# A second layer of seven products for one more block of four rounds, an earlier first FFT stage, and logits copied on ScalarE

## The chip, the cores and the metric

The kernel runs on one core of a Trainium2 chip. A core has five engines with a queue of instructions each: TensorE (PE, matrix products; its weight loads are shown apart as PEld), VectorE (DVE), ScalarE (ACT), GpSimd (POOL) and SyncE (SP, which issues most transfers here). Operands lie in SBUF, 128 partitions wide; products land in PSUM. The metric is the device time of one execution in microseconds. It was 1263.31 us before the change, the median of three runs (1263.24 to 1265.31).

## The reference

The input `x` has 8 batches of 2496 rows of 256 numbers. First the real part of a two-dimensional Fourier transform of each batch; then a layer of eight experts, of which each row takes the one with the greatest logit.

```python
X = np.fft.fft(x, axis=1)
X = np.fft.fft(X, axis=2)
x = X.real.astype(np.float32).reshape(B * S, D)        # 19968 x 256

logits = x @ w_gate                                    # 256 x 8
expert_idx = np.argmax(logits, axis=1)
probs = np.exp(logits - logits.max(-1, keepdims=True))
probs /= probs.sum(-1, keepdims=True) + 1e-09
gate_w = probs[np.arange(N), expert_idx]
for e in range(E):                                     # the rows of expert e
    h = np.maximum(x_sorted[lo:hi] @ w1[e], 0.0)       # 256 -> 1024
    y_sorted[lo:hi] = h @ w2[e]                        # 1024 -> 256
return gate_w[:, None] * y                             # in the order of the rows
```

No row is dropped: an expert's share of rows depends on the data, so the kernel finds out on the chip which rows go to which expert.

## The kernel before

**The transform** of a batch has two stages. The first, `first(b)`, goes through three thirds of the batch: a transfer brings `xq` (L289), DVE folds it (`fold`, with L295 to L297 in `fold_d` and L306), TensorE multiplies (`s`, L316 on), ScalarE copies the result (`t`, L321), and SP writes it to `Td` in HBM (L342). `regroup` (L351) reads it back in another order, as two tiles `t`. The second stage, `second(b)`, turns one column (`turn_last`: a product `pr`, and the copy `t` by ScalarE on L372), runs nine groups (`group`: two products `p` from `t` and the table, and ScalarE's copy `zz`, L379), and from these ten tiles of 128 places: two products `p` from `zz`, ScalarE's copy `zs` (L405), ScalarE's `mirror` (L384), the copy of the logits `lg` (L408), and two additions on DVE into `rows` (L410). Each place gives two rows of the transform. After five tiles `route` (L416) finds each row's expert, gate and place; `send` then writes rows to their places in the sorted array `Xs` in HBM by an indirect transfer on POOL (L236), 128 rows each, behind two tiny copies (ScalarE's `due`, L468, and POOL's cast, L469).

**The plan.** When a batch has been routed, `plan` (L478) works out on one partition of DVE how many full blocks of rows each expert has, and writes a table of where each block begins and whose weights it takes. Its arrays have 21 entries (`MOST`), the greatest number of blocks that any call plans. SP reads the table and fetches rows (`fetch_rows`, L526) and weights (`fetch_weights`, L542), up to three blocks ahead.

**The experts** go in rounds, one per batch. From batch 2 a round has blocks of 512 rows: three in round 2, five in rounds 3 to 6; round 7 has five and then smaller ones. A block, written (round, index), has two layers. The plain form of the first layer is a chain of products `ph`, that of the second 4 times 16 products `py` with a scaling by ScalarE (L891) and an indirect store after each. Blocks for which `halved` holds (512 rows from round 3 on) run the first layer as seven products of half the size in place of eight (`seven`, L614; products a to e; Strassen's scheme), for which DVE prepares sums of the weights (`Left`, L552) and of the turned rows (`right`, L568, called by `turn`, L577, which also transposes on L583 and negates on ScalarE on L586). Blocks for which `quartered` holds run the second layer so too: `lower` (L660), with the sums of weights by `Below` (L594, its subtractions on L607; on POOL for blocks of 512) and sums of the hidden tile by DVE (chores on L819 at the end of `seven`, `s2` on L870, `s4` on L874). In `lower` DVE adds the products (L705, L707, L713 and `plus`, L683) and ScalarE scales them (`scaled`, L679). `Below` of a block is begun during the block before if that one's second layer is direct (`soon`, L855), else in the block's own first layer. `quartered` holds for index 3 and 4 of rounds 3 to 6 and for the whole of round 7.

**The order.** Every engine's queue is in the order in which the program was written; nothing is reordered later. The main loop (L996 on) goes through the steps of the experts' work (`work`), and after each takes some ticks from the side work, `mixed(b)` (L935): the first stage of batch b + 1 (`ahead_of`) and the second stage of batch b, then the plans (`close`). So a round's blocks carry the transform of the next batches between their products: a generator step of the first stage comes with every second step of the second. 12 further ticks (`AHEAD`) of the round after next come at the end of a round, and in rounds 3 to 5 they fall into the second layer of index 2. PSUM gives the transform three banks (tag `m`, `pm_`), so that at most three of its results are unread at any time.

Of the kernel before, what the change touches and what calls it, by code (L numbers as in the profile page):

```python
# [15 lines left out]
ALU = mybir.AluOpType  # L16
ACTF = mybir.ActivationFunctionType
AX_X = mybir.AxisListType.X
PSUM = bass.MemoryType.PSUM

B, S, D = 8, 2496, 256
# [14 lines left out]
E, F = 8, 1024  # L36
# [6 lines left out]
NY = H + 1  # L43
# [7 lines left out]
def bc(ap, axis, n):  # L51
    shape = list(ap.shape)
    shape.insert(axis, n)
    return ap[tuple([slice(None)] * axis + [None])].to_broadcast(shape)
# [136 lines left out]
def halved(b, size):  # L191

    return size == 512 and b > 2 or size == 256 and b == B - 1


def quartered(b, size, at):

    return halved(b, size) and (b == B - 1 or at >= 3)


def block_consts():
# [14 lines left out]
def kernel(ctx: ExitStack, tc, x, w_gate, w1, w2, out):  # L216
# [52 lines left out]
    con, k = {}, 0  # L269
# [91 lines left out]
    def second(b):  # L361

        t4 = None

        def turn_last(h):

            nonlocal t4
            t4 = ahead.pop((b, "t4", h))
            n = min(HALF, NG - h * HALF)
            pr = pm_.tile([GP, HALF], F32, tag="m", name="pr")  # L370
            mm(pr[:, 0:n], con["rot"][:], t4[0:GP, 0:n, H])
            act.copy(t4[0:GP, 0:n, H], pr[:, 0:n])  # L372

        def group(g):
            i, n = g % HALF, LAST if g == NG - 1 else GP
            p2 = pm_.tile([128, 2, n], F32, tag="m", name="p2")
            for c in range(2):
                mm(p2[:, c], t4[0:GP, i, c * H:(c + 1) * H], con["m2"][:, c, 0:n])
            act.copy(zz[:, :, g * GP:g * GP + n], p2[:])  # L379
            if g == HALF - 1:  # L380
                turn_last(1)

        def mirror(rows, k):
            act.copy(free(rows[:], (k + 1) * W + D - 1, [-W, 2], [-1, H - 1]),  # L384
                     free(rows[:], k * W + 1, [W, 2], [1, H - 1]))

        turn_last(0)
        yield
        group(0)
        yield  # L390
        group(1)
        yield
        for h in range(2):
            rows = sp.tile([128, NSL, W], F32, tag="rows", name="rows")
            lg = sp.tile([128, NSL, E], F32, tag="lg", name="lg")
            for i in range(HW):
                w, k = HW * h + i, 2 * i
                if w + 2 < NG:
                    group(w + 2)
                p3 = pm_.tile([128, 2 * NY + 2 * E + 1], F32, tag="m", name="p3")  # L400
                z = zz[:, :, 128 * w:128 * (w + 1)]
                mm(p3[:, 0:NY + 2 * E], z[:, 0], con["rd"][:, 0, 0:NY + 2 * E], True, False, skip_group_check=True)
                mm(p3[:, NY:], z[:, 1], con["rd"][:, 1], False, True, skip_group_check=True)
                zs = sp.tile([128, NY + 1], F32, tag="zs", name="zs")
                act.copy(zs[:], p3[:, NY + 2 * E:])  # L405
                if i:
                    mirror(rows, k - 2)
                vec.tensor_copy(lg[:, k:k + 2], p3[:, NY:NY + 2 * E].rearrange("p (m e) -> p m e", m=2))  # L408
                for m, op in enumerate((ALU.add, ALU.subtract)):
                    vec.scalar_tensor_tensor(rows[:, k + m, 0:NY], p3[:, 0:NY], zs[:, 0:1], zs[:, 1:],  # L410
                                             op0=ALU.add, op1=op)
                yield
            mirror(rows, k)
            yield from route(b, h, rows, lg)
# [63 lines left out]
    def plan(b, size, k, last):  # L478

        nonlocal gone  # L480

        def one(name, *dims, dt=F32):
            return cp.tile([1, *dims], dt, tag="p_" + name, name="p_" + name, bufs=2 if name == "gone" else 1)

        nb, ni = one("nb", E), one("ni", E, dt=I32)
        ce, ex, rb, n = one("ce", E), one("ex", E), one("rb", E), one("n", E)
        lo = one("lo", E, E)
        vec.tensor_tensor(nb[:], base[0:1], gone[:], op=ALU.subtract)
        vec.tensor_scalar(ni[:], nb[:], size - 1.0 if last else 0.0, None, op0=ALU.add)
        vec.tensor_scalar(ni[:], ni[:], size.bit_length() - 1, None, op0=ALU.logical_shift_right)  # L490
        vec.tensor_copy(nb[:], ni[:])
        vec.tensor_tensor(lo[:], bk["low"].rearrange("p (a b) -> p a b", a=E), bc(nb[:], 1, E), op=ALU.mult)
        vec.reduce_sum(ce[:], lo[:], axis=AX_X)
        vec.tensor_tensor(ex[:], ce[:], nb[:], op=ALU.subtract)
        yield
        vec.scalar_tensor_tensor(rb[:], ex[:], -float(size), gone[:], op0=ALU.mult, op1=ALU.add)
        ge, ei = one("ge", MOST, E), one("ei", MOST)
        val, eq, rw = one("val", MOST, E + 1), one("eq", MOST, E + 1), one("rw", MOST)
        vec.tensor_tensor(ge[:], bc(bk["i"], 2, E), bc(ce[:], 1, MOST), op=ALU.is_ge)
        vec.reduce_sum(ei[:], ge[:], axis=AX_X)  # L500
        yield
        vec.tensor_tensor(eq[:], bc(ei[:], 2, E + 1), bc(bk["e9"], 1, MOST), op=ALU.is_equal)
        vec.memset(val[:, :, E:E + 1], float(E * CAP))
        vec.scalar_tensor_tensor(val[:, :, 0:E], bc(bk["i"], 2, E), float(size), bc(rb[:], 1, MOST),
                                 op0=ALU.mult, op1=ALU.add)
        yield
        vec.tensor_tensor(val[:], val[:], eq[:], op=ALU.mult)
        vec.reduce_sum(rw[:], val[:], axis=AX_X)
        tab = cp.tile([1, 2, MOST], I32, tag="p_tab", name="p_tab", bufs=4)
        vec.tensor_copy(tab[:, 0], rw[:])  # L510
        vec.tensor_scalar(tab[:, 1], ei[:], E - 1.0, None, op0=ALU.min)
        if last:
            cnt = cp.tile([1, 1], I32, name="cnt")
            vec.tensor_copy(cnt[:], ce[:, E - 1:E])
            tabs["cnt"] = cnt
        if not last:

            vec.tensor_scalar(n[:], ex[:], -1.0, float(k), op0=ALU.mult, op1=ALU.add)
            vec.scalar_tensor_tensor(n[:], n[:], 0.0, nb[:], op0=ALU.max, op1=ALU.min)
            nxt = one("gone", E)  # L520
            vec.scalar_tensor_tensor(nxt[:], n[:], float(size), gone[:], op0=ALU.mult, op1=ALU.add)
            gone = nxt
        yield
        tabs[b, size, last] = tab
# [410 lines left out]
    def mixed(b):  # L935

        one, two = (ahead_of(b + 1) if b + 1 < B else iter(())), second(b)
        for _ in range(3):
            next(one, None)
            yield  # L940
        for k, _ in enumerate(two):
            if k % 2:
                next(one, None)
            yield
        yield from woven(close(b), one)
        yield from through(b)
# [133 lines left out]
```

## Time and profile before

| what | us |
|---|---|
| median of three runs | 1263.31 |
| the profiled execution | 1264.13 |
| its span | 1262.3 |
| TensorE busy | 1214.1 |
| DVE busy | 777.0 |
| POOL busy | 446.1 |
| ScalarE busy | 424.8 |

A profile is of one execution. The span runs from its first instruction to its last; busy times are of instructions that compute, and those of a pipelined engine overlap at their edges. Lines of groups give a source line, engine, operation, output and inputs, then the busy time and the mean of one in ns, then the idle time before them and what ended most of it. L221 is the helper through which all matrix products go, so that these are told apart by the names of their tiles. Where a line says `<-ACT t L372` the engine stood until that instruction was done. The windows give the busy time of each engine in a stretch. The mean granted clock of TensorE in this execution was 0.971.

### The profile page before, as it was taken

How to read it: one execution, taken by the hardware profiler on the slowest of the kernel's cores; microseconds unless marked ns; L12 is line 12 of the kernel's file. 1: busy time of each engine (PE TensorE's matmuls, PEld its weight loads, DVE VectorE, ACT ScalarE, POOL GpSimd, SP SyncE). 2: the span in 40 equal slices, each digit the busy share in tenths (PEclk: the TensorE clock that was granted, in tenths of full speed). 3: DMA queues.
4: the chain of work that ended last, by engine and by line, in shares of the span. 5: the costliest groups of instructions: out<-in, count | busy, mean ns of one | idle time of the engine just before them, and what ended most of it. 6: DMA issues, size and time to landing. Idle time of an engine off the chain costs nothing.

```text
span 1262.3 us, 22196 instructions
## 1 busy us (share of the span) xinstructions
PE 1214.1 (96%) x7289; PEld 1080.3 (86%) x7289; DVE 777.0 (62%) x1884; ACT 424.8 (34%) x1087; POOL 446.1 (35%) x527
## 2 busy tenths in 40 slices
PE   5769999999999999999999999999999999999997
PEld 3658988777788899888988898889999999999996
DVE  4546334443466788576866578686888784444663
ACT  1423332332243433433344333432333232222222
POOL 0245436154116512472225603472364241111112
PEclk6759999999999999999999999999999999999998
DMA  8869898765348454573336435453346338788887
GB/s 236 272 195 327 304 307 306 204 224 169 126 147 258 138 142 160 154 263 115 101 123 207 141 94 160 140 179 101 105 138 190 109 105 282 284 289 275 285 284 278
DMA packets 163216, 249.79 MB, mean 198 GB/s; under 512 B 118601, under 2 KB 130227, under 8 KB 143516
## 3 DMA queue, kind: packets, MB, share of 16 engines
q1 hardware_dynamic: 146327, 203.28, 51.0%
q0 software_dynamic: 15888, 42.14, 9.3%
q10 hardware_dynamic: 885, 2.94, 0.7%
q8 instruction: 59, 0.97, 0.3%
q14 instruction: 57, 0.47, 0.1%
HBM read 194.91 MB, written 54.83 MB: 198 GB/s over the span
## 4 chain that ended last, share of the span: by engine, by line
PE 62%; issue 17%; DVE 10%; DMA 5%; POOL 4%; ACT 2%; POOLq 0%; SPq 0%; DVEq 0%; ACTq 0%
PE py L221 18%; PE a L221 9%; PE c L221 7%; PE ph L221 6%; PE p L221 6%; PE b L221 5%; PE d L221 4%; PE s L221 3%; PE e L221 3%; POOL out_dram L236 3%; DMA t<-Td 1%; DMA xq<-in_x_dram 1%; POOL Xs L236 1%; DVE xT L583 1%; DMA Td<-t 1%
## 5 line engine op out<-in xcount | busy, mean ns | idle before, releaser
L236 POOL DMA_INDIRECT out_dram<-y,ro x163 | 160.9, 987 | 629.5 <-ACT y L679 299.6
L221 PE MATMUL py<-w_sb,hT 128*128 128x256 f32 x1504 | 340.3, 380 | 0.0
L221 PEld LDWEIGHTS py<-w_sb,hT 128*128 128x128 f32 x1504 | 281.2, 190 | 36.9 <-issue 1.0
L236 POOL DMA_INDIRECT Xs<-rows,pi x160 | 164.2, 1026 | 111.7 <-DVE rows L410 53.0
L221 PE MATMUL ph<-xT,w_sb 128*128 128x128 f32 (+2 forms) x992 | 173.1, 330 | 10.0 <-DVE ro L792 8.8
L221 PEld LDWEIGHTS ph<-xT,w_sb 128*128 128x128 f32 x992 | 137.6, 194 | 34.4 <-issue 16.5
L221 PE MATMUL a<-xT,w_sb 128*128 128x256 f32 (+1 forms) x512 | 117.9, 357 | 0.0
L837 DVE TENSOR_SCALAR hT<-ph 128x512 f32<-128x512 f32 x43 | 29.7, 691 | 127.9 <-PE ph L221 68.2
L586 ACT ACTIVATE xT<-xT 128x256 f32<-128x256 f32 (+1 forms) x94 | 36.5, 388 | 181.7 <-DVE xT L583 137.3
L221 PEld LDWEIGHTS a<-xT,w_sb 128*128 128x128 f32 x512 | 88.5, 190 | 10.0 <-DVE xT L583 0.3
L891 ACT ACTIVATE y<-py,xb 128x256 f32<-128x256 f32 x94 | 44.5, 473 | 153.8 <-PE py L221 152.1
L635 DVE TENSOR_TENSOR hT<-hT,b 128x512 f32<-128x512 f32 x57 | 39.2, 687 | 79.0 <-PE b L221 53.4
L408 DVE COPY lg<-p 128x16 f32<-128x16 f32 x80 | 13.8, 173 | 111.4 <-ACT zs L405 111.3
L645 ACT ACTIVATE hT<-a 128x512 f32<-128x512 f32 x57 | 34.0, 597 | 134.1 <-PE a L221 131.1
L221 PE MATMUL s<-xq,w 104*112 104x256 f32 (+2 forms) x208 | 62.4, 425 | 11.8 <-DVE xq L297 9.5
L469 POOL CAST pi<-due 128x1 int32<-128x1 f32 x140 | 42.2, 302 | 68.4 <-ACT due L468 68.4
L221 PE MATMUL a<-w_sb,hT 128*128 128x128 f32 x528 | 66.0, 276 | 0.0
L221 PEld LDWEIGHTS p<-table,t 120*128 120x128 f32 x352 | 54.7, 206 | 10.6 <-issue 3.1
L221 PEld LDWEIGHTS a<-w_sb,hT 128*128 128x128 f32 x528 | 63.1, 192 | 0.7
L221 PE MATMUL c<-xT,ws 128*128 128x256 f32 (+1 forms) x256 | 60.2, 362 | 1.2 <-DVE hT L641 0.4
L221 PE MATMUL p<-table,zz 128*128 128x145 f32 (+1 forms) x320 | 57.6, 306 | 3.6 <-DVE rows L410 2.4
L583 DVE STREAM_TRANSPOSE xT<-xb 128x512 f32<-128x512 f32 (+1 forms) x91 | 56.3, 631 | 7.0 <-DMA xb<-Xs 7.0
(149 smaller groups left out, 2103.2 us busy)
## 6 DMA issues: line engine op xcount, KB each, us to landing
w_sb<-in_moe_w_dram SPq DMA_DIRECT2D x132, 1024.0 KB, 6.9
xq<-in_x_dram SPq DMA_DIRECT2D x24, 896.0 KB, 8.9
xb<-Xs SPq DMA_DIRECT2D x112, 128.0 KB, 3.3
Td<-t SPq DMA_DIRECT2D x18, 448.0 KB, 3.3
t<-Td SPq DMA_DIRECT2D x8, 768.0 KB, 7.0
t<-Td SPq DMA_DIRECT2D x8, 640.0 KB, 9.3
xb<-Xs SPq DMA_DIRECT2D x52, 64.0 KB, 4.7
xb<-Xs SPq DMA_DIRECT2D x88, 32.0 KB, 4.8
```

The lines of the kernel that those rows point to most:

```text
L221: nc.tensor.matmul(o, lhsT=lhsT, rhs=rhs, start=start, stop=stop, **kw)
L236: return unordered(pool.indirect_dma_start(out=dst, out_offset=bass.IndirectOffsetOnAxis(ap=idx, axis=0), in_=rows, in_offset=None, bounds ...
L408: vec.tensor_copy(lg[:, k:k + 2], p3[:, NY:NY + 2 * E].rearrange("p (m e) -> p m e", m=2))
L469: pool.tensor_copy(idx, due[:])
L583: vec.transpose(free(xT[:], 256 * h, [32, n // 32], [BIG, 2], [1, 32]), free(xb, 512 * h, [64, n // 32], [1, 2], [2, 32]))
L586: act.activation(odd, odd, ACTF.Copy, scale=-1.0)
L635: vec.tensor_tensor(h12, h11, b[:], op=add)
L645: act.activation(h11, a[:], ACTF.Relu)
L837: vec.tensor_scalar(o, ph[:], 0.0, None, op0=ALU.max)
L891: act.activation(y[:, i % 2], py[:], ACTF.Copy, scale=meta[:, i, 1:2])
```

## The change

Five parts. `quartered` now also holds for index 2 of rounds 3 to 6: four blocks of 512 rows run their second layer as seven products, 64 `py` instructions each giving way to 112 shorter ones, with the sums on DVE that belong to them; their `Below` is begun during index 1 (whose second layer is direct), and that of index 3 in its own first layer. In `second`, the copy of the logits goes from DVE to ScalarE, behind the mirror. `plan` uses arrays of `k` entries, the number of blocks of that call, where it used 21. In `mixed`, the first stage is advanced at the even steps of the second stage, the first one included, where it was at the odd ones. By this each step of the first stage comes one tick earlier, and in SP's queue the two reads of `regroup` come ahead of the next fetch of rows and weights.

```diff
--- before.py
+++ after.py
@@ -195,7 +195,7 @@
 
 def quartered(b, size, at):
 
-    return halved(b, size) and (b == B - 1 or at >= 3)
+    return halved(b, size) and (b == B - 1 or at >= 2)
 
 
 def block_consts():
@@ -405,7 +405,7 @@
                 act.copy(zs[:], p3[:, NY + 2 * E:])
                 if i:
                     mirror(rows, k - 2)
-                vec.tensor_copy(lg[:, k:k + 2], p3[:, NY:NY + 2 * E].rearrange("p (m e) -> p m e", m=2))
+                act.copy(lg[:, k:k + 2], p3[:, NY:NY + 2 * E].rearrange("p (m e) -> p m e", m=2))
                 for m, op in enumerate((ALU.add, ALU.subtract)):
                     vec.scalar_tensor_tensor(rows[:, k + m, 0:NY], p3[:, 0:NY], zs[:, 0:1], zs[:, 1:],
                                              op0=ALU.add, op1=op)
@@ -494,21 +494,22 @@
         vec.tensor_tensor(ex[:], ce[:], nb[:], op=ALU.subtract)
         yield
         vec.scalar_tensor_tensor(rb[:], ex[:], -float(size), gone[:], op0=ALU.mult, op1=ALU.add)
-        ge, ei = one("ge", MOST, E), one("ei", MOST)
-        val, eq, rw = one("val", MOST, E + 1), one("eq", MOST, E + 1), one("rw", MOST)
-        vec.tensor_tensor(ge[:], bc(bk["i"], 2, E), bc(ce[:], 1, MOST), op=ALU.is_ge)
-        vec.reduce_sum(ei[:], ge[:], axis=AX_X)
-        yield
-        vec.tensor_tensor(eq[:], bc(ei[:], 2, E + 1), bc(bk["e9"], 1, MOST), op=ALU.is_equal)
+        ge, val, eq = (one(name, MOST, E + 1)[:, 0:k] for name in ("ge", "val", "eq"))
+        ei, rw = (one(name, MOST)[:, 0:k] for name in ("ei", "rw"))
+        count = bk["i"][:, 0:k]
+        vec.tensor_tensor(ge[:, :, 0:E], bc(count, 2, E), bc(ce[:], 1, k), op=ALU.is_ge)
+        vec.reduce_sum(ei, ge[:, :, 0:E], axis=AX_X)
+        yield
+        vec.tensor_tensor(eq, bc(ei, 2, E + 1), bc(bk["e9"], 1, k), op=ALU.is_equal)
         vec.memset(val[:, :, E:E + 1], float(E * CAP))
-        vec.scalar_tensor_tensor(val[:, :, 0:E], bc(bk["i"], 2, E), float(size), bc(rb[:], 1, MOST),
+        vec.scalar_tensor_tensor(val[:, :, 0:E], bc(count, 2, E), float(size), bc(rb[:], 1, k),
                                  op0=ALU.mult, op1=ALU.add)
         yield
-        vec.tensor_tensor(val[:], val[:], eq[:], op=ALU.mult)
-        vec.reduce_sum(rw[:], val[:], axis=AX_X)
+        vec.tensor_tensor(val, val, eq, op=ALU.mult)
+        vec.reduce_sum(rw, val, axis=AX_X)
         tab = cp.tile([1, 2, MOST], I32, tag="p_tab", name="p_tab", bufs=4)
-        vec.tensor_copy(tab[:, 0], rw[:])
-        vec.tensor_scalar(tab[:, 1], ei[:], E - 1.0, None, op0=ALU.min)
+        vec.tensor_copy(tab[:, 0, 0:k], rw)
+        vec.tensor_scalar(tab[:, 1, 0:k], ei, E - 1.0, None, op0=ALU.min)
         if last:
             cnt = cp.tile([1, 1], I32, name="cnt")
             vec.tensor_copy(cnt[:], ce[:, E - 1:E])
@@ -939,7 +940,7 @@
             next(one, None)
             yield
         for k, _ in enumerate(two):
-            if k % 2:
+            if k % 2 == 0:
                 next(one, None)
             yield
         yield from woven(close(b), one)
```

## The prediction

> **What bounds the kernel now.** The page's busy rows come first.
>
> ```profile
> PE 1214.1 (96%) x7289; PEld 1080.3 (86%) x7289; DVE 777.0 (62%) x1884; ACT 424.8 (34%) x1087; POOL 446.1 (35%) x527
> ...
> PE   5769999999999999999999999999999999999997
> ...
> PEclk6759999999999999999999999999999999999998
> ```
>
> TensorE is busy for 96% of the span and at nine tenths or more in every slice from the fifth to the last but one; the granted clock is below nine tenths only in the first three slices and the last. So what counts is TensorE's own work and the few places where it stands. The list of TensorE's waits from 87 us on names those:
>
> ```profile
> PE ph L221 <- DVE ro L792: 8.8, 1, 8.8
> PE pr L221 <- DMA t<-Td: 2.3, 1, 2.3
> PE p L221 <- ACT t L372: 1.7, 3, 0.8
> PE ph L221 <- DVE hT L837: 1.2, 1, 1.2
> ```
>
> Columns: total us, times, longest. By the timeline they lie at 78.6 to 87.4 (the first expert block waits for rows), at 211.6, at 425.6 and 571.3 (the second layer of the third block of rounds 3 and 4: this change's place), and at 121.3. Next, the price of a second layer, by groups:
>
> ```profile
> L221 PE MATMUL py<-w_sb,hT 128*128 128x256 f32 x1504 | 340.3, 380 | 0.0
> ...
> L221 PE MATMUL a<-w_sb,hT 128*128 128x128 f32 x528 | 66.0, 276 | 0.0
> ```
>
> The means overlap (matmuls are pipelined), so I price by spacing: a direct second layer of 512 rows runs from 391.43 to 405.24, 13.81 us for 64 `py` instructions; a product of the seven (16 instructions) takes 454.16 to 455.94, 1.785 us, seven of them 12.50. Last, the windows: a direct second layer (3, 1), the one to be changed (3, 2) (rounds 3 and 5), one by sevens (3, 3), and round 6's at index 1 and the whole block at index 2.
>
> ```profile
> core 0: us, PE busy (x) PEld busy (x) DVE busy (x) ACT busy (x) POOL busy (x), PEclk, DMA share, GB/s
> 391.40:405.20 13.80, 13.80 (x65) 12.15 (x65) 8.76 (x35) 4.00 (x13) 8.85 (x14) 1.00 0.82 302
> 417.30:439.30 22.00, 21.13 (x117) 18.80 (x117) 15.82 (x26) 8.73 (x24) 10.77 (x11) 1.00 0.18 61
> 451.40:464.90 13.50, 13.50 (x122) 13.47 (x122) 12.71 (x33) 3.80 (x10) 0.00 (x0) 1.00 0.17 73
> ...
> 708.70:727.60 18.90, 18.90 (x110) 17.24 (x109) 9.12 (x17) 7.83 (x22) 9.95 (x10) 1.00 0.15 55
> 821.80:835.60 13.80, 13.80 (x66) 12.15 (x65) 12.45 (x53) 4.01 (x13) 8.92 (x14) 1.00 0.25 90
> 835.60:862.00 26.40, 26.16 (x121) 22.72 (x120) 20.47 (x42) 9.17 (x22) 20.03 (x23) 1.00 0.53 162
> ```
>
> In the sevens window DVE is busy for 12.7 of 13.5 us and TensorE still does not stand. But (3, 2) also carries a dozen ticks of the next batch's FFT, which TensorE, ScalarE and DVE must pass through in a written order.
>
> **The second layer by sevens, four blocks (index 2 of rounds 3 to 6).** TensorE's own saving is 13.81 - 12.50 = 1.31 us a block, 5.3 in all. Against it stand new waits. In (3, 2) the order becomes: product a, b, a, `pr`, d, first `p` group, its second half, c, `p`, `s`, e, `p`, tile `p`, `p`, tile `p`, `s`, last c, and the rest. Two of ScalarE's results are now late.
>
> First, the copy `t` (L372), for which the second half of the first `p` group waits. In ScalarE's queue it stands behind the negation of `xT` (L586), which waits for a DVE transpose (L583). Today all engines show there:
>
> ```profile
> 424.34 0.70 DVE L583 STREAM_TRANSPOSE xT<-xb 128x512 f32<-128x512 f32 x1
> ...
> 425.07 0.42 ACT L586 ACTIVATE xT<-xT 128x256 f32<-128x256 f32 x1 [3.61 <-DVE xT L583]
> 425.39 0.15 ACT L372 COPY t<-pr 120x6 f32<-120x6 f32 x1
> ...
> 425.60 0.37 PE L221 MATMUL p<-table,t 120*128 120x120 f32 x1 [0.76 <-ACT t L372]
> ```
>
> By sevens DVE does more ahead of that transpose. I place it with (3, 3)'s spacings, T = 0 at the first product: the chore pair (L819) to 2.2, `s2` (L870) to 3.45, a fold of the next batch (1.18 + 0.69 + 0.68 + 0.17, less overlaps) to 5.9, `s4` (L874), which needs the third product (3 x 1.785 = 5.36), to 7.1, a `Left` subtraction to 7.7, transpose to 8.4, L586 to 8.75, L372 to 8.96. TensorE arrives at 5.36 + 0.14 + 1.785 + 0.22 = 7.5 and stands 1.46. Second, after e the `p` tile waits for a `zz` copy (L379), queued on ScalarE behind both scalings of `y` (L679), which wait for DVE's sum of e and b (L713, L684), and that stands behind four `xs` subtractions (L571 to L574, 0.42 each) and a fold. TensorE leaves c at 11.0, e at 14.06 and reaches the tile at 14.06 + 2 x 0.44 + 0.51 = 15.45; DVE has L705, L707, a `Left` step and `xs` to 13.6, the fold, L713 at 15.5, L684 to 16.4, ScalarE two `y` to 17.3 and `zz` to 17.65: 2.3 standing. Then 0.3 on the last `pr` and 0.85 on the last tile, again behind `y`. Sum of stands 4.9; clean work 12.5 + 6.68 (from the groups: `pr` 2 x 0.14, `p` 6 x 0.44, tiles 4 x 0.51, `s` 2 x 0.86) = 19.2; together 24.05 against 22.01 today. **+2.05 each in rounds 3 and 4.** I leave out that (3, 2) today has 0.76 of side work that these prices don't explain; with it, 24.8.
>
> Round 5 has no `s` and no fold: the same chain with `s4` at 5.5 gives stands of 1.15, 1.86, 0.35 and 0.8, hence 12.5 + 4.96 + 4.16 = 21.6 against 18.93: **+2.7.** Round 6 has no side work. It saves 1.31, and the 0.41 by which (6, 2) (26.40) is longer than its siblings with direct layers (25.99) may go with its POOL additions. But these now run in (6, 1), where DVE has 12.45 of 13.8 us filled with plans; additions on POOL stretch DVE's instructions on two SBUF inputs (L573 lasted 1.91 instead of 0.42 beside one, L295 1.52 to 1.64 instead of 0.69), some 1.2 us for each of four. Between -1.85 (all hidden) and +1 (half of the 4.8 beyond the spare 1.35, less the saving): **-0.4**, near the middle.
>
> The block behind one by sevens runs its first group slower: (3, 4) 6.34 us, its successor 6.40, against 6.04 behind a direct one. Four times 0.35: **+1.4**. The `ws2` additions of index 3, formerly prepared on POOL during index 2, now fall in its own first layer, as (3, 4)'s do, which is 24.89 long: nothing. In rounds 3 to 5 the moved additions lie on POOL beside (3, 1), 8.85 of 13.8 filled with sends; 5.1 more end at about 405.7 and are needed at 419, and DVE has 5.0 us free for its 4.8 lost. Nothing.
>
> **The first stage a step earlier.** One tick earlier for each batch, its `xq` loads (896 KB each) and `Td` stores included; SP's `t` loads come ahead of the next rows and weights instead of behind. At 211.6 TensorE waited for such a load:
>
> ```profile
> 211.60 0.37 PE L221 MATMUL pr<-t,table 120*120 120x6 f32 x2 [2.32 <-DMA t<-Td]
> ```
>
> It had been issued at 199.72, behind row loads to 196.3 and weights to 198.0. Moved ahead by a tick, it should be in time: **-2.3** (bounds 0, if the store to HBM is late itself, and -2.32). The rows and weights that SP now issues after it have 15 to 25 us in hand by their issue and first use, and cost nothing; without that cover a load of 7 us (the median of the `t` loads) would be the price.
>
> **Shorter plans.** Six or seven operations on 168 to 189 elements (L499 to L508, 296 to 343 ns) shrink to those on 64 or so (207 to 218): about 0.1 each, 0.65 a plan. Only the plan at 116 to 120.4 had TensorE waiting (1.15): **-0.6** (0 to -1.15). The others lie in DVE's free time.
>
> **Logits on ScalarE.** 80 copies of 173 ns leave DVE. Queued behind the mirror they come later:
>
> ```profile
> 433.12 0.27 ACT L405 COPY zs<-p 128x130 f32<-128x130 f32 x1 [0.43 <-PE p L221]
> 433.36 0.40 ACT L384 COPY rows<-rows 128x254 f32<-128x254 f32 x1
> ```
>
> and both additions of rows (L410) now wait for them: about 0.35 later a tile (0.41 of mirror and a copy, less the DVE copy and overlaps). ScalarE's small copies take 168 ns (L372) and 188 (L468), so the instruction itself costs the same. At the start this chain leads to the first sends: **+0.35** (-0.2 to +1.5). Later tiles have a bank of three and the plan's time in hand; **+0.5** (0 to +2) for the third tiles of the woven rounds.
>
> Here a rule speaks for the change. The Trainium skill, "Perfetto Trace Analysis", section "Optimizing Scalar/DVE Operations", gives an access overhead in PSUM of some 125 ns on DVE and 51 ns on ScalarE, and says that a saturated DVE may hand work over; by that, an estimate, 80 x 74 ns = 5.9 us would be saved, on no critical path. The rows show no such difference (173 against 168 to 188).
>
> **Sum:** 2 x 2.05 + 2.7 - 0.4 + 1.4 = +7.8; -2.3 - 0.6 + 0.35 + 0.5 = -2.05; together +5.75. The profiled execution took 1264.13 (span 1262.3 and 1.83 around it), 0.8 above the median of 1263.31, so **1269.0**. What a measurement can tell from no change is 0.2%, 2.5 us.
>
> **The rivals.**
> *No new stands (faster, 0.20).* TensorE stays full as in 451 to 465, where DVE had 12.7 of 13.5 filled and did not delay it. For it: (3, 2) gives DVE and ScalarE 19 us, and TensorE's queue may be served later than my order by hand assumes. Against it: two DVE chains ahead of ScalarE's queue. It decides if L684 ends before TensorE reaches the tile, 1.3 us sooner than I have it (17.65 less 16.3, where the first stand is kept). Then -5.3 + 1.4 - 2.05: 1257.4; without the slower first groups 1256.
> *Half of the stands (same, 0.12).* Either only the `t` or only the `zz` wait is real: +7.8 less 6 to 7, near 1262.5.
> *Contention (slower, 0.13).* The additions moved into index 1 stretch DVE and hold sends: POOL would be 8.85 + 5.1 = 14.0 of 13.8 filled, so ScalarE's `due` copies, eight buffers deep, may stop and hold its queue. Today's rows show no ScalarE wait of this kind; 1 us a round, and +1 in round 6: 1273 to 1274.
> A rule sharpens it: the Trainium skill, "SBUF — State Buffer", section "Who interferes with whom", has a DVE instruction with two SBUF inputs blocked for the whole of a GpSimd instruction that reads SBUF, and the reverse. By it the four additions cost DVE at most 4 x 1.28 = 5.1 us a block, an estimate; that is past the 5.0 free by a hair, against the rows' 4.8.
> *Regroup in the way (inside the first case).* The `t` load ahead delays rows by up to 7 us; hidden.
>
> **How the numbers follow.** My forecast 0.55, with its own range 1265.5 to 1272; contention 0.13; half 0.12; no stands 0.20. Slower 0.68, same 0.12, faster 0.20. Below 1257 and above 1274 I leave about one in ten each: 1257 to 1274.
>
> **What would show it.** Sevens' `a` group at 592 instead of 528 and `py` at 1248; new TensorE waits `<-ACT t L372` of about 1.5 and `<-ACT zz L379` of about 2.3 in index 2 of rounds 3 to 5, second layers of 24 and 21.6 us; first groups of 6.35 in index 3; no 2.3 wait at 211. I am wrong if these second layers come in under 21 us, or if the wait list after 130 us stays under 2 us in all.

## The result, and the profile after

The changed kernel took 1279.69 us, the median of four executions (1279.0 to 1283.79); the kernel before took 1264.31 beside it. The ratio is 1.0134, with a 95% interval of 1.0115 to 1.0152: slower by 15.4 us. The forecast was 1269.0, in a range of 1257 to 1274. The sign was right; the size was not, and the time lies above the range.

The profiled execution took 1279.0 (span 1276.9). First its page, the busy rows, the slices of TensorE and of its clock:

```profile
PE 1211.9 (95%) x7481; PEld 1083.3 (85%) x7481; DVE 803.2 (63%) x1860; ACT 426.6 (33%) x1171; POOL 467.9 (37%) x543
...
PE   6769999999999899998999999989999999999996
...
PEclk9869999999999999999999999999999999999998
```

TensorE has 2.2 us less to do than before (1211.9 against 1214.1) and stands longer. Where before there were only nines, three slices have an eight (14, 19 and 27 of 40). The list of its waits from 60 us on says for whom:

```profile
PE c L221 <- DVE hT L642: 10.0, 3, 5.5
PE ph L221 <- DVE xT L584: 8.0, 1, 8.0
PE p L221 <- ACT zz L379: 7.5, 7, 2.1
...
PE p L221 <- ACT t L372: 3.5, 5, 1.3
```

The waits for `zz` and for `t` are the two that were forecast. The largest, three waits of product c for DVE's L642 in first layers, was not. (Lines behind the plan are one higher here than before: L642 was L641.) The wait of 2.3 us for a `t` load at 211.6 is gone. The products by sevens have the count expected of the change:

```profile
L221 PE MATMUL py<-w_sb,hT 128*128 128x256 f32 x1248 | 282.0, 380 | 0.3
...
L221 PE MATMUL a<-w_sb,hT 128*128 128x128 f32 x656 | 81.6, 276 | 0.0
```

`py` fell by 256. Group a rose by 128 and not by the 64 that the prediction named, since two of the seven products share this tile. The windows of the same places as before (from the top: second layers of (3, 1) and (3, 2), first and second of (3, 3), second of (5, 2) and (6, 1), first of (6, 2)):

```profile
core 0: us, PE busy (x) PEld busy (x) DVE busy (x) ACT busy (x) POOL busy (x), PEclk, DMA share, GB/s
386.20:400.40 14.20, 14.07 (x65) 12.07 (x64) 11.59 (x35) 3.81 (x13) 9.60 (x13) 1.00 0.70 234
412.50:436.60 24.10, 20.25 (x165) 19.29 (x164) 18.23 (x37) 8.29 (x28) 10.92 (x12) 1.00 0.25 81
436.60:451.20 14.60, 12.35 (x58) 10.58 (x57) 12.17 (x19) 4.68 (x10) 6.43 (x5) 1.00 0.77 236
451.20:465.50 14.30, 14.30 (x125) 14.12 (x125) 12.66 (x31) 4.36 (x12) 0.00 (x0) 1.00 0.00 1
713.70:734.90 21.20, 18.59 (x158) 17.95 (x157) 13.40 (x29) 7.31 (x26) 8.46 (x11) 1.00 0.17 57
828.70:842.80 14.10, 14.05 (x65) 12.07 (x64) 12.92 (x44) 3.87 (x13) 9.26 (x13) 1.00 0.17 64
842.80:862.10 19.30, 13.76 (x57) 11.58 (x57) 15.95 (x37) 5.11 (x14) 13.82 (x20) 0.91 0.67 207
```

In (3, 2) TensorE is busy for 20.25 of 24.1 us, in the first layer of (6, 2) for 13.76 of 19.3, and there alone the granted clock is not full.

A table of layers, made from the starts of their first products in each timeline, shows where the time went. The last columns are of three kernels described below: the sevens alone, the changed kernel without them, and the one with its three faults mended.

| layer | before | after | sevens alone | without sevens | mended |
|---|---|---|---|---|---|
| start of (3, 0) | 344.45 | 340.13 | 342.79 | 339.80 | 339.18 |
| (3, 1) second | 13.81 | 14.21 | 14.77 | 13.81 | 13.82 |
| (3, 2) second | 22.01 | 24.12 | 23.04 | 21.87 | 20.66 |
| (3, 3) first | 12.09 | 14.60 | 12.09 | 12.19 | 12.32 |
| (3, 3) second | 13.44 | 14.31 | 13.45 | 14.32 | 14.31 |
| (4, 0) second | 22.72 | 21.85 | 22.72 | 21.84 | 21.84 |
| (5, 2) second | 18.93 | 21.16 | 21.08 | 18.93 | 18.71 |
| (6, 2) first | 12.59 | 19.30 | 21.53 | 12.08 | 12.90 |
| (6, 2) second | 13.81 | 12.50 | 12.50 | 13.82 | 12.51 |
| (6, 3) first | 12.09 | 12.44 | 12.43 | 12.08 | 12.56 |
| (3, 0) to (7, 0) | 567.09 | 584.39 | 582.92 | 565.56 | 562.96 |

Layer by layer round 4 repeats round 3 within 0.1 us, before and after, but for the first layer of index 0 (12.44 against 12.09 in both kernels). Up to round 3 the changed kernel gains 4.3 us in these two profiles; from there to round 7 it loses 17.3; the last 1.6 of this execution are at its very end, where the last scaling of `y` waited 4.05 us for a store, before 1.98. The start of (3, 0) varies from one execution to the next: seven of the profiled kernels are the same program up to there as the changed one and have it between 339.18 and 342.42, and the kernel before and the one with the sevens alone, alike up to there too, at 344.45 and 342.79. What follows it can be compared far more closely.

### The profile page after: what moved, and what is told of

Same layout as the page of the kernel before. It is cut to its first block, busy times and chain, and to the rows that moved or that the text cites. A ratio compares the mean times of both kernels' runs of the same rounds, so it can differ in the third digit from the quotient of the medians.

```text
span 1276.9 us, 22783 instructions
## 1 busy us (share of the span) xinstructions
PE 1211.9 (95%) x7481; PEld 1083.3 (85%) x7481; DVE 803.2 (63%) x1860; ACT 426.6 (33%) x1171; POOL 467.9 (37%) x543
## 5 line engine op out<-in xcount | busy, mean ns | idle before, releaser
L221 PE MATMUL py<-w_sb,hT 128*128 128x256 f32 x1248 | 282.0, 380 | 0.3
L221 PEld LDWEIGHTS py<-w_sb,hT 128*128 128x128 f32 x1248 | 233.2, 190 | 32.4 <-ACT y L892 1.9
L236 POOL DMA_INDIRECT Xs<-rows,pi x160 | 167.3, 1046 | 109.9 <-ACT lg L408 53.2
L410 DVE SCALAR_TENSOR_TENSOR rows<-p,zs 128x129 f32<-128x129 f32 x160 | 48.8, 347 | 118.1 <-ACT lg L408 113.3
L221 PE MATMUL a<-w_sb,hT 128*128 128x128 f32 x656 | 81.6, 276 | 0.0
L221 PEld LDWEIGHTS a<-w_sb,hT 128*128 128x128 f32 x656 | 78.4, 192 | 0.9
L221 PE MATMUL s<-xq,w 104*112 104x256 f32 (+2 forms) x208 | 62.7, 425 | 15.4 <-DVE xq L297 10.9
L636 DVE TENSOR_TENSOR hT<-hT,b 128x512 f32<-128x512 f32 x57 | 39.1, 687 | 59.5 <-PE b L221 34.2
L892 ACT ACTIVATE y<-py,xb 128x256 f32<-128x256 f32 x78 | 36.9, 474 | 118.5 <-PE py L221 118.3
L221 PEld LDWEIGHTS c<-xT,ws 128*128 128x128 f32 x256 | 43.7, 192 | 22.3 <-DVE hT L642 17.7
## 6 DMA issues: line engine op xcount, KB each, us to landing
xq<-in_x_dram SPq DMA_DIRECT2D x24, 896.0 KB, 12.2
```

The source lines that it names most:

```text
L221: nc.tensor.matmul(o, lhsT=lhsT, rhs=rhs, start=start, stop=stop, **kw)
L236: return unordered(pool.indirect_dma_start(out=dst, out_offset=bass.IndirectOffsetOnAxis(ap=idx, axis=0), in_=rows, in_offset=None, bounds ...
L636: vec.tensor_tensor(h12, h11, b[:], op=add)
L892: act.activation(y[:, i % 2], py[:], ACTF.Copy, scale=meta[:, i, 1:2])
```

## The experiments

Theory A: the loss is the second layer by sevens, through ScalarE's order in index 2 and through POOL's weight subtractions, which stretch DVE's instructions where DVE is late already. Rivals stand with each run.

**The sevens alone.** The kernel before with

```diff
-    return halved(b, size) and (b == B - 1 or at >= 3)
+    return halved(b, size) and (b == B - 1 or at >= 2)
```

> The kernel before with one line changed: index 2 of rounds 3 to 6 by sevens, nothing else. From 344 us of the profile before to the last blocks the changed kernel takes 17.3 us more, up to there 4.3 us less. Theory A (the whole loss is the second layer by sevens and what it does to DVE and POOL around it): 1264.3 + 17.3, near 1281.6, with second layers of index 2 of about 24.1 us in rounds 3 and 4, 21.2 in round 5, and first layers of 14.6 (index 3, rounds 3 and 4) and 19 (index 2, round 6). Rival B (the logits on ScalarE and the earlier first stage share the guilt, since they put more ahead of the zz copies): clearly less, 1272 to 1276, with shorter second layers.

Measured: 1280.86 (1278.51 to 1284.0), ratio 1.0138 (1.0111 to 1.0164). So the loss is that of the sevens. The places were only partly those expected: index 2 takes 23.0 in rounds 3 and 4, index 3's first layer does not stand at all (12.09), but index 1 loses 0.9 in each round and the first layer of (6, 2) 8.9 instead of 6.7.

**The changed kernel without the sevens** (the same line back to `at >= 3`).

> The changed kernel with index 2 back to the direct second layer, so the earlier first stage, the logits on ScalarE and the shorter plans alone. Theory A: the 4.3 us gained by 344 us remain and nothing is lost later: near 1260.0, faster than before by 0.3%. Rival B: 1266 or more, for the stands in rounds 3 to 5 stay in part.

Measured: 1259.79 (1258.1 to 1261.48), ratio 0.9968 (0.9955 to 0.9980). The other parts gain 4.4 us, as expected. The two effects, +16.7 and -4.4, sum to 12.3; the change as a whole costs 15.4. The difference of 3 is not clear of the intervals, but the profiles have it too: from (3, 0) to (7, 0) the sevens alone lose 15.8 and the other parts gain 1.5, which makes 14.3, and the change loses 17.3. So the parts act on each other. The table shows one place for it: the first layer of (3, 3), 14.60 with both, and 12.1 to 12.2 with either alone.

**Sevens at index 2 of round 6 only.**

```diff
-    return halved(b, size) and (b == B - 1 or at >= 2)
+    return halved(b, size) and (b == B - 1 or at >= 3 or at == 2 and b == B - 2)
```

> The changed kernel with index 2 by sevens in round 6 alone. Round 6 has no side work in index 2. Theory A: the run of the changed kernel without sevens plus 6.1 us (index 1 +0.3, first layer of index 2 +6.7, its second layer -1.3, index 3 +0.35): near 1266. Rival (as the prediction had it, -0.4): near 1259.6.

Measured: 1268.63 (1266.73 to 1270.48), ratio 1.0039 (1.0028 to 1.0051): 8.8 above the kernel without sevens, where theory A had 6.1 and the prediction -0.4. One block by sevens, with no side work in it, costs 8.8 of the 19.9 us that all four cost in the changed kernel (1279.69 less 1259.79). Its first layer took 20.15 us.

**What stands in round 6.** DVE's timeline of the changed kernel around the start of (6, 2), five of its instructions:

```profile
830.98 1.93 DVE L451 TENSOR_TENSOR pos<-pos,oh 128x80 f32<-128x80 f32 x1
...
834.92 1.91 DVE L494 TENSOR_TENSOR p_ex<-p_ce,p_nb 1x8 f32<-1x8 f32 x1
...
843.08 2.05 DVE L505 SCALAR_TENSOR_TENSOR p_val<-bt,p_rb 1x56 f32<-1x56 f32 x1
...
847.14 1.89 DVE L490 TENSOR_SCALAR p_ni<-p_ni 1x8 int32<-1x8 int32 x1
...
851.41 0.67 DVE L636 TENSOR_TENSOR hT<-hT,b 128x512 f32<-128x512 f32 x1
```

and POOL's timeline of the same time:

```profile
831.50 1.29 POOL L608 TENSOR_TENSOR ws<-w_sb 128x512 f32<-128x512 f32 x1
...
835.51 1.29 POOL L608 TENSOR_TENSOR ws<-w_sb,ws 128x512 f32<-128x512 f32 x1
...
843.77 1.28 POOL L608 TENSOR_TENSOR ws<-w_sb,ws 128x512 f32<-128x512 f32 x1
...
847.73 1.27 POOL L608 TENSOR_TENSOR w_sb<-w_sb 128x512 f32<-128x512 f32 x1
```

Each of the four subtractions on POOL falls within one tiny DVE instruction of the plan or the route, and that one takes 1.89 to 2.05 us, where the same lines took 0.15 to 0.29 undisturbed in the profile before. That is 7.0 us of DVE lost, the four times less the 0.15 to 0.24 that they take undisturbed in these shapes, and the first addition of the block (L636) comes at 851.41, 8.6 us after the block's start; before, it came 3.3 us after (838.87 against 835.6). TensorE can run ahead only as far as its five tiles reach, and stands 5.54. The same four subtractions on DVE:

```diff
-                    soon = Below(got[0][1], pool)
+                    soon = Below(got[0][1], vec if follow[0] == B - 2 and follow[3] == 2 else pool)
```

> The changed kernel with the four weight subtractions for index 2 of round 6 on DVE instead of POOL. They are 0.69 us each on DVE, 2.7 in all; on POOL they held four tiny DVE instructions of the plans for 1.89 to 2.05 us each, 7.0 us lost. Theory A (the collision of POOL's subtractions with DVE's instructions is what makes DVE late there): the first layer of index 2 gets some 4.3 us shorter, 15 instead of 19.3, total near 1275.4. Rival C (DVE simply has too much to do there, the long durations are waits that would come anyway): 2.7 us longer, near 1282.4.

Measured: 1273.33 (1271.98 to 1274.85), ratio 1.0068 (1.0043 to 1.0092): 6.4 us less than the change, 2 more than expected. DVE's timeline of this kernel:

```profile
844.49 0.67 DVE L608 TENSOR_TENSOR w_sb<-w_sb 128x512 f32<-128x512 f32 x1
...
845.47 0.16 DVE L490 TENSOR_SCALAR p_ni<-p_ni 1x8 int32<-1x8 int32 x1
...
847.91 0.67 DVE L636 TENSOR_TENSOR hT<-hT,b 128x512 f32<-128x512 f32 x1
```

L490 is back at 0.16, L636 comes 3.7 us after the block's start (844.24), the first layer takes 12.99. DVE does 2.7 us more work and is earlier by 4.9 all the same: rival C is out.

**ScalarE's order in index 2.** The timeline of all engines of the changed kernel shows both forecast waits:

```profile
421.00 0.42 ACT L587 ACTIVATE xT<-xT 128x256 f32<-128x256 f32 x1 [6.12 <-DVE xT L584]
421.32 0.15 ACT L372 COPY t<-pr 120x6 f32<-120x6 f32 x1
...
421.53 0.37 PE L221 MATMUL p<-table,t 120*128 120x120 f32 x1 [1.27 <-ACT t L372]
...
429.12 0.91 ACT L680 ACTIVATE y<-y,xb 128x256 f32<-128x256 f32 x2 [3.39 <-DVE y L684]
...
429.94 0.34 ACT L379 COPY zz<-p 128x240 f32<-128x240 f32 x1
...
430.33 0.39 PE L221 MATMUL p<-table,zz 128*128 128x145 f32 x1 [2.05 <-ACT zz L379]
```

ScalarE sits idle for 6.12 and 3.39 us ahead of an instruction that waits for DVE, with the short copy that TensorE needs in the queue behind it. A kernel that issues the scalings, and the turning of the next block, a step later:

```diff
         s4()
         step()
-        turn_some()
+        if nt == 1:
+            turn_some()
         yield
...
         plus(u2, e)
-        scaled(0, 0, D)
-        send_rows(0)
         step()
+        if nt == 2:
+            turn_some()
         yield
+        scaled(0, 0, D)
+        send_rows(0)
         c = bank("c")
         product(2, c)
         plus(u2, c)
-        scaled(1, H, D)
-        send_rows(1)
         step()
         yield
+        scaled(1, H, D)
+        send_rows(1)
         yield
```

> The changed kernel with two things moved in the second layer by sevens of 512 rows: both scalings of y (L680) with their stores are issued one step later, behind the side work's zz copies, and the two transposes and the xs subtractions one step later, so that the copy t (L372) has no xT negation ahead of it in ScalarE's queue. Theory A (ScalarE's order makes the stands of 1.27, 2.05 and 0.43 in rounds 3 and 4 and 0.45, 1.63 and 0.43 in round 5): they go, second layers of index 2 of 20.4, 20.4 and 18.7 us instead of 24.1, 24.1 and 21.2, 10.0 us in all, near 1269.7. Rival D (DVE is full there, and the stands only move to the next thing that waits for it): over 22.5 us for rounds 3 and 4, total above 1275.

Measured: 1277.71 (1276.98 to 1278.3), ratio 1.0099 (1.0083 to 1.0116), 2.0 less than the change and 8 more than expected. In index 2 the waits on `t` and `zz` above 0.3 us are gone; its second layers take 21.05, 21.05 and 19.48, some 0.7 more than expected, and in place of the three waits stands one of 0.8 to 0.9 for rows (L410). But the gain was spent elsewhere: the `xs` subtractions, a step later too, end in the next block's first layer. DVE's timeline at the start of (3, 4):

```profile
463.71 0.43 DVE L572 TENSOR_TENSOR xs<-xT 128x256 f32<-128x256 f32 x1
464.25 0.43 DVE L573 TENSOR_TENSOR xs<-xT,xs 128x256 f32<-128x256 f32 x1
464.71 0.42 DVE L574 TENSOR_TENSOR xs<-xT,xs 128x256 f32<-128x256 f32 x1
```

TensorE begins that block at 463.38 and its product b waits for L573. Thirteen blocks have this wait of 0.3 to 0.4, and their first layers are longer than in the changed kernel: eleven by 0.6 (12.99 against 12.38 here), (7, 0) by 0.8 and (7, 1) by 1.4, 8.9 us in all. By its total the run fits rival D; by the layers theory A held for index 2, and the edit had a cost of its own that I had not priced. (In the mended kernel below the `xs` subtractions stay where they were, and (3, 4) takes 12.38 again.)

**Index 3.** The timeline of the changed kernel at the start of (3, 3), the fold of the next batch's last third and the cast of the block's row numbers:

```profile
437.17 1.29 POOL L608 TENSOR_TENSOR ws<-w_sb 128x512 f32<-128x512 f32 x1
...
438.55 3.43 POOL L608 TENSOR_TENSOR ws<-w_sb,ws 128x512 f32<-128x512 f32 x2
...
438.75 1.24 DVE L297 COPY pm<-xq 104x2 f32<-104x2 f32 x1
...
440.77 1.23 DVE L793 CAST ro<-xb 128x4 int32<-128x4 f32 x1
...
444.23 1.13 PE L221 MATMUL c<-xT,ws 128*128 128x256 f32 x4 [2.25 <-DVE hT L642]
```

With that block's subtractions on DVE, in the second half of its first layer:

```diff
+                late = size == BIG and at == 3 and b < B - 1
-                below, soon = soon or Below(w2_sb, pool if size == BIG else vec), None
+                below, soon = soon or Below(w2_sb, pool if size == BIG and not late else vec), None
...
-                for _ in seven(size, left.all, xT, hT, both, step, ends):
-                    if both:
+                for j, _ in enumerate(seven(size, left.all, xT, hT, both, step, ends)):
+                    if both and (j >= 7 or not late):
                         below.step()
```

> The changed kernel with the four weight subtractions for index 3 of rounds 3 to 6 on DVE in the second half of that block's first layer, instead of on POOL at its beginning. Theory A (in rounds 3 and 4 POOL's subtractions meet DVE's folds and the cast ro, 0.25 + 1.06 + 1.05 us lost, and this makes most of the 2.25 that TensorE stands): the stand shrinks to about 0.3, the first layers of index 3 to 12.2 to 13.2 us instead of 14.6, minus 3 to 4.5 in all, near 1275.5. Rival E (the late rows and folds, in the order of DVE's queue, are the cause): still about 2 us of stand, and 2.7 us of subtractions more on DVE, total 1279 to 1284.

Measured: 1278.63 (1277.94 to 1279.63), ratio 1.0108 (1.0091 to 1.0125), 1.1 less than the change. By the total this would be near rival E; by the trace it is theory A. DVE's timeline of this kernel:

```profile
442.44 0.17 DVE L297 COPY pm<-xq 104x2 f32<-104x2 f32 x1
...
443.38 0.17 DVE L793 CAST ro<-xb 128x4 int32<-128x4 f32 x1
```

The two take 0.17 again, the wait for L642 is gone in rounds 3 and 4, and the first layers take 12.32 instead of 14.60. In the profiled execution the gain is hidden by two second layers of index 2 of 25.78 instead of 24.12: the granted clock fell there after the wait for `zz`, which this kernel still has (below). That the other executions lost it in the same way was not seen, since they have no trace.

What brings the fold to that place? The changed kernel with the logits back on DVE (`vec.tensor_copy` in place of `act.copy` on L408):

> The changed kernel with the logits back on DVE. In the kernel with sevens alone the first layer of index 3 did not stand (12.09), in the changed one it does (14.6). If the earlier first stage does that, which brings the fold of the last third of the batch to that place: still 14.3 to 14.6, total near 1279. If the logits on ScalarE do it (rows later): 12.1 to 12.5, near 1275.

Measured: 1280.28 (1276.04 to 1284.54), ratio 1.0125 (1.0091 to 1.0159), first layers of index 3 of 14.67. So it is not the logits. In the kernel with sevens alone no fold stands at the start of (3, 3), and of the parts that are left only the earlier first stage moves a fold in DVE's queue: the shorter plans have as many steps as before. The sevens with the earlier first stage and nothing else were not run.

**The other parts, each alone on the kernel before.** The earlier first stage, `if k % 2 == 0:` in `mixed`:

> The kernel before with the first stage at the even steps, nothing else. The prediction has -2.3 for it (the stand of 2.32 at 211.6). Read from the runs so far: 3.0 less in the block at 203.9, and further gains and losses of 0.9 in rounds 3 to 6 (index 0 shorter, the second layer of index 3 longer), together -3 to -3.5: near 1261.

Measured: 1259.92 (1258.44 to 1262.42), ratio 0.9965 (0.9945 to 0.9984). In its timeline the first layer at 205.1 takes 9.45 instead of 12.47.

> The kernel before with the logits copied by ScalarE, nothing else. The prediction has +0.35 at the start and +0.5 in the woven rounds: near 1265. If all that the kernel without sevens gains (4.4) is the earlier first stage (3.3) and the shorter plans (1.05), this is 0: near 1264.2.

Measured: 1264.09 (1262.49 to 1268.74), ratio 1.0002 (0.9990 to 1.0015): nothing, as the second reading said.

> The kernel before with the shorter plans alone. The prediction has -0.6. TensorE's wait at 121 us gets 1.05 shorter in every kernel that has them: near 1263.1.

(The edit is the part of the change's diff in `plan`.) Measured: 1260.91 (1260.16 to 1263.95), ratio 0.9979 (0.9965 to 0.9993): -3.0, more than either figure. The wait at 121 us shrinks by 0.7 (1.15 to 0.43) and the first layer of (6, 2) by 0.5 (12.59 to 12.09). A third part seems to lie at the start, before the first expert block. The waits for rows (L410) there do not show it: the longest shrinks from 2.45 to 1.38, but the two sum to 2.6 before and 2.7 with the shorter plans. The waits from 60 us on, before:

```profile
PE p L221 <- DVE rows L410: 2.6, 2, 2.4
...
PE ph L221 <- DVE hT L837: 1.2, 1, 1.2
```

and with the shorter plans:

```profile
PE p L221 <- DVE rows L410: 2.7, 2, 1.4
...
PE ph L221 <- DVE hT L838: 0.4, 1, 0.4
```

What shows it are the 20 indirect stores of batch 0: from the first's start to the last's they take 25.33 us instead of 26.67 (26.67 in the kernel with the sevens alone too); with the earlier first stage 26.05 with the shorter plans, 27.83 without. That the plan for batch 0 makes this difference was not tested by itself.

**Both good parts together**, the earlier first stage and the shorter plans, index 2 direct and the logits on DVE:

> The kernel before with the earlier first stage and the shorter plans alone (direct second layer at index 2, logits on DVE). From the runs so far: -4.0 for the first, -1.05 for the plan whose end TensorE waited for: near 1259.0, about 0.4% faster than before.

Measured: 1257.25 (1256.84 to 1258.15), ratio 0.9942 (0.9926 to 0.9959), 6.7 us faster than before and the lowest median of all. The changed kernel without the sevens differs from this one by the logits alone and gained 4.4; the two intervals overlap, and from (3, 0) to (7, 0) the profiles are 0.2 apart (565.37 and 565.56), so whether the logits on ScalarE cost something in this company stays open.

**The change with its three faults mended.** The scalings as above; the first transpose at the start of the next step, the others where they were; the subtractions for index 2 and index 3 of rounds 3 to 6 on DVE:

```diff
         s4()
         step()
-        turn_some()
+        if nt == 1:
+            turn_some()
         yield
+        if nt == 2:
+            turn_some()
         product(6, d)
...
-                    soon = Below(got[0][1], pool)
+                    soon = Below(got[0][1], vec)
```

> The changed kernel with its sevens kept and the three suspected causes mended together: the scalings of y one step later, behind the zz copies, the first transpose behind the copy t, but the xs subtractions where they were; the weight subtractions for index 2 and for index 3 of rounds 3 to 6 on DVE. Theory A (these three hold the loss): second layers of index 1 of 13.8, of index 2 of 21.1, 21.1 and 19.5 us, first layers of index 3 of 12.3, of index 2 of round 6 of 13.0; the sevens then gain about 0.75 in rounds 3 and 4, lose 0.5 in round 5 and nothing in round 6, so near the kernel without sevens: 1259. If something else of weight is left, 1265 or more.

Measured: 1258.99 (1257.58 to 1260.06), ratio 0.9958 (0.9942 to 0.9974). All layers named come in as expected or better (20.66 in (3, 2), 18.71 in (5, 2)). So the three causes hold all of the loss that a total can tell: the sevens, mended, cost nothing against the kernel without them (1259.79). From round 3 to round 7 they even gain 2.6 us (562.96 against 565.56), and lose 1.6 of it in the first layer of (7, 0), 14.06 us against 12.43, with two waits for L642 of 0.43 and 0.60. There POOL still makes the subtractions, and between the two waits one of them meets an addition of weights on DVE:

```profile
907.78 2.47 DVE L567 TENSOR_TENSOR ws<-w_sb 128x512 f32<-128x512 f32 x1
```

```profile
908.40 1.29 POOL L608 TENSOR_TENSOR ws<-w_sb 128x512 f32<-128x512 f32 x1
```

This instruction took 0.72 in the kernel without sevens. So the second wait follows a collision of the same kind, in a place that the repair left; what made DVE late for the first was not found.

## Why the prediction was right or wrong

The step that failed is the price of POOL's weight subtractions where they meet DVE: -0.4 for round 6, and "nothing" for index 1 and for the first layers of index 3. Set against the kernel without sevens, layer by layer in the profiles, the four blocks cost 18.8 us from (3, 0) to (7, 0): 6.7 in the second layers of index 2, which the forecast had at 6.8 against the kernel before; -0.35 in the first layer of (5, 4); 4.8 in the first layers of index 3; 1.0 in index 1 of rounds 3 to 5; and 6.6 in round 6. For the last three kinds of layer, 12.4 us, the forecast had -0.4, and +1.4 for slower groups. The runs with these subtractions on DVE take nearly all of the 12.4 away: the first layers of index 3 fall to 12.3, the second layers of index 1 to 13.81, and round 6 as a whole takes 132.6 us, as without sevens (132.66), instead of 139.25.

**ScalarE's order in index 2: right.** Forecast 24.05 us for the second layers in rounds 3 and 4, and 21.6 in round 5; measured 24.12, 24.12 and 21.16. The stands were 1.27, 2.05 and 0.43, where the forecast had 1.46, 2.3, 0.3 and 0.85. Even an instant fits: the transpose ends at 420.97, 8.45 us after the layer's start at 412.52, placed by hand at 8.4. The rival without stands is refuted by these waits. That the times of the layers fit so well is in part luck: the stands sum to 3.75 and not to 4.9 (in round 5 to 2.5 and not 4.2), and the rest of the layer takes 20.4 and not 19.2 (18.65 and not 17.5). The working had seen 0.76 of side work that its prices did not explain, and left it out. Its stand for the tile is also 2.2 by its own numbers (17.65 less 15.45), not 2.3, and the 16.3 in the rival without stands does not follow from them.

**"Nothing" for the subtractions of index 3 in its own first layer: wrong, +2.5 in rounds 3 and 4 each.** I took (3, 4) as the row for it, where no fold lies. The change moves a fold to the start of (3, 3), and I followed the earlier first stage on SP's queue and at 211 us but not on DVE's in rounds 3 and 4. The interplay of two parts of the change was in no step.

**Round 6, -0.4: wrong, the largest miss.** The mechanism was named and priced, at 4.8 us of DVE of which half would show. It cost 7.0 us of DVE: 1.7 to 1.9 for each of the four, since a DVE instruction of 0.15 to 0.24 that meets a subtraction of 1.28 did not end before it. Nor did all four run in (6, 1), as the forecast had it: two stood on POOL behind sends and met DVE in the first layer of (6, 2), where the block's own additions were due. The upper end, +1, rested on halving and on a mean of 1.2; the lower end, -1.85, should have been -1.7 (1.31 and 0.41). The mean came from rows with two inputs in SBUF. The profile before has dearer ones, with one input; on DVE and on POOL:

```profile
856.42 1.95 DVE L792 CAST ro<-xb 128x4 int32<-128x4 f32 x1
```

```profile
857.05 1.28 POOL L607 TENSOR_TENSOR ws<-w_sb,ws 128x512 f32<-128x512 f32 x1
```

This cast takes 0.34 at 838.80 in the same profile. Against the kernel without sevens round 6 lost 7.2 in the first layer, of which 5.54 is the stand and the rest mostly the clock after it, +0.3 in index 1, -1.3 in the second layer, +0.35 in index 3: +6.6.

**"Nothing" in index 1 of rounds 3 to 5: wrong by 0.3 to 0.4 a round.** DVE has 11.59 us filled instead of 8.76. I had compared its sums with the length of the layer; but the transposes it delays stand ahead of ScalarE's scaling of `y`, and that one frees TensorE's bank. In the kernel with sevens alone this is 0.9 a round, with waits `<-ACT y` of 0.6 to 0.7.

**The slower first group, +1.4: mostly wrong.** Only (6, 3) shows the 0.35; (5, 3) takes 12.09 behind a block by sevens. In rounds 3 and 4 the larger wait covers it in the changed kernel, but with the sevens alone these layers take 12.09 too, as before.

**The earlier first stage, -2.3: right in kind, too small;** it gave -4.0 alone. The wait at 211.6 went, and with it 3.0 in that block; the rest of the profile moved by amounts that I had not worked out: 0.87 less in the second layer of index 0 of rounds 3 to 5 (22.72 to 21.85), 0.87 more in that of index 3 of rounds 3 and 4 (13.44 to 14.31), so that round 5 alone keeps the gain.

**The shorter plans, -0.6: too small;** -3.0 (the interval reaches from -4.4 to -0.9). "The others lie in DVE's free time" was wrong for round 6's, and seemingly for batch 0's.

**The logits on ScalarE, +0.85: too large;** nothing measurable. The rule about PSUM overheads that I set against the rows had no gain to show either.

In all, the forecast's +7.8 for the sevens was +16.7 alone, its -2.05 for the rest was -4.4, and the interplay, some 3 by the profiles, stood in no term. The contention rival (1273 to 1274) had the right mechanism with too low a price. The range ended at 1274 because its upper case took 1 us a round for that mechanism, where one round alone took over 6.

## What to carry to other kernels

Work moved to an idle engine is not free where the two engines get in each other's way: price it per collision, by the whole length of the longer instruction if the profile shows such rows, and count how many collisions fall where the other engine is late already. When a change has several parts, follow each moved piece of work into the place where another part moves something too. In an in-order queue, a short copy that the bottleneck needs must not be issued behind an instruction that waits for a third engine; but the piece moved out of its way has its own due time, and it has to be checked before it is moved.

## What the runs showed of the hardware

**After a stand the clock of TensorE can drop to half, even after 2 us.** Behind the stand of 5.54 us in round 6 the windows of the changed kernel show (columns as above; the granted clock is the third number from the end)

```profile
848.00:853.60 5.60, 0.18 (x1) 0.00 (x0) 5.15 (x16) 0.60 (x1) 4.46 (x7) 0.96 0.96 336
853.70:856.00 2.30, 2.28 (x5) 1.85 (x6) 1.39 (x3) 0.71 (x2) 1.80 (x3) 0.50 0.89 349
856.00:860.00 4.00, 4.00 (x19) 3.48 (x18) 2.76 (x5) 1.36 (x4) 1.61 (x4) 0.93 0.12 42
```

2.3 us at a granted clock of 0.50. Behind the shorter stand for `zz` it is not always so. The kernel with the logits back on DVE has this stand in rounds 3 and 4, 2.04 and 2.05 us long, in the same place of the same code, and behind it, in two windows of 3.7 us:

```profile
430.30:434.00 3.70, 3.70 (x17) 3.38 (x16) 1.06 (x5) 1.26 (x3) 0.97 (x1) 0.54 0.42 136
```

```profile
582.30:586.00 3.70, 3.70 (x31) 3.55 (x30) 1.69 (x6) 1.51 (x4) 1.06 (x2) 1.00 0.47 156
```

Round 3 ran at 0.54, round 4 at 1.00; the layers took 25.68 and 24.04 us. So a stand can cost 1.64 us more than its length, and whether it does changes within one execution. The Trainium skill, "TensorE: Matmul & The Clock Gate", section "Part 1: The HAM clock gate (the "warmup" mystery)", explains the half clock by an activity window of about 3.4 us that runs freely, whatever the kernel does. If so, what a stand does would depend on where it falls in that window. The change between rounds 3 and 4 fits that, but the stand of 2.05 is shorter than an idle window, and what was counted as idle no run here shows.

**A collision with a subtraction on POOL can hold a DVE instruction until POOL's ends, even for eight numbers.** A 1x8 instruction took 1.91 us beside a POOL subtraction of 1.29 and one with a single input 1.89, where 0.15 to 0.16 is usual. By the timelines above these two began 0.6 us before POOL's instruction and ended with it: that DVE had begun did not help it. Not every DVE instruction is held: in the same profile L636, which adds a product in PSUM to `hT`, ran from 473.95 wholly beside two subtractions on POOL (473.14 to 476.10) and took its usual 0.69.
